# Moving v down the partitions, copies inside SBUF to SyncE, and masks to GpSimd in an attention and feed-forward kernel

## The chip, the core and the metric

The kernel runs on one core of a Trainium2 chip. A core has TensorE (matrix products into PSUM), VectorE and ScalarE (element work on SBUF and PSUM), GpSimd (element work on SBUF, and the issue of loads that convert types), SyncE (the issue of other transfers) and 16 DMA engines. Each engine works through its own list in order, and semaphores connect them. The metric is the device time of one execution in microseconds, as a median of several runs.

## The reference

Four batches of eight heads, 768 positions, 64 numbers a head. Each position attends to its neighbours closer than 16 and to one summary of every block of 32: the maximum of the block's k, and the mean of its v. The result, 3,072 rows of 512, goes through a feed-forward part with a hard-swish.

```python
k_sum = k.reshape(B, H, nb, block, D).max(axis=3)
v_sum = v.reshape(B, H, nb, block, D).mean(axis=3)
scores_l = scale * np.matmul(q, k.transpose(0, 1, 3, 2))        # kept where |i - j| < 16
scores_s = scale * np.einsum('bhsd,bhnd->bhsn', q, k_sum) + np.log(block)
a = softmax(concatenate([masked scores_l, scores_s]))
x = a @ concatenate([v, v_sum])                                  # (3072, 512)
h = x @ w_in                                                     # (512, 2048)
out = (h * clip(h + 3, 0, 6) / 6) @ w_out                        # (2048, 512)
```

## The kernel before

**Attention.** A batch is cut into 12 query blocks of 64. The queries are shifted by 16, so that block t needs the keys of positions 64t to 64t + 95. `kaug[p]` (p is one of four pairs of heads) holds for each block 96 key columns and the 24 block maxima, 120 in all; one matmul gives 64 queries' scores against all 120 (`scores`, L519). ScalarE takes the exponential into `at` (L527), VectorE multiplies the 96 neighbour rows by a band mask (L531; for the first half of batch 0 a bias is added on TensorE instead). `vaug` holds for each block the 120 rows of v that answer to these: on partitions 0 to 63 the block's own rows, on 64 to 95 the 32 rows ahead, which are the next block's first rows (the halo), on 96 to 119 the 24 block sums, the same for every block; a 65th column of ones gives the softmax's denominator. Its rows are 66 numbers apart. `values` (L632) multiplies `at` with `vaug`; `finish` divides (L663, L667), transposes on TensorE (L682) and copies to `x`.

**Where the rows come from.** For batch 0, k and q are loaded by rows (`knat`, `qnat`) and transposed on TensorE (L448, L493). For batches 1 to 3 they are loaded in squares of 32 into `kraw` (four loads, L367) and, shifted by 16 rows, into `qraw` (eight half loads, L375), of which there is one each, and VectorE transposes them (`turn`, L588, L592), with the third piece of each key window copied from the next. v is loaded by L385 in four loads a batch. For batch 0 the halo is copied by VectorE and ScalarE (`halo`, L406), for the others it is loaded from HBM a second time (`load_vhalo`, L393). The block sums are matmuls with an indicator (`vsum_first` L552, `vsum` L567); they are spread to all 12 blocks by copies for batches 0 and 1, by SyncE transfers from SBUF to SBUF for 2 and 3 (L575).

**Feed-forward.** Half a batch (384 rows) at a time: 16 tiles of `h` (four matmuls each, L700), drained by ScalarE (L705) and VectorE (L707) into `g`; then 128 rows of output with 16 matmuls (L720), an eviction to `ot` (L432) and a store (L730). The tiles go through three PSUM banks `h`, one bank `o`, and two pairs of banks `S` for attention.

**Order.** The order of the work is written out by hand in `ORDER`, a list of some 1,500 operations. `K10.0` is the load of batch 1's raw k, first part; `Q..` a load of q, `V..` of v, `I`, `O` of the weights, `H` the halo, `z` in the changed kernel a zero fill; `k`, `q`, `s`, `u`, `v`, `w` are the steps `k_step`, `q_step`, `scores`, the block sums, `values` and `turn`; `F` and `G` the two feed-forward products; `:A` and `:D` name the engine where there is a choice. `Plan.run` goes through the list with estimated durations to choose buffers, and each engine gets its operations in that order. In the first 22 us of that plan, matmuls on a constant tile (L803) fill TensorE's gaps.

```python
def load_v(b, c, prio):                          # L381
    op("POOL", 0.95, lambda: nc.gpsimd.dma_start(out=o[0:QB, lo:hi, 0:D], in_=rows[:, lo:hi]),
       w=[("v", b % 2, c)], prio=prio, dma=1.7)
```

Of the kernel before, what the change touches and what calls it, by code (L numbers as in the profile page):

```python
# [9 lines left out]
F32 = mybir.dt.float32  # L10
# [5 lines left out]
D = 64  # L16
BLK = 32
# [4 lines left out]
VW = 66  # L22
# [7 lines left out]
c.0 K00.0 c.7 K01.0 c.10 c.11 c.12 c.13 c.9 c.1 Q000.0 K02.0 Q010.0 c.2 c.3 k00.0 k01.0 q010.0 k01.1 k01.4 k00.1 q010.1:A  # L30
k00.4 c.4 k00.3:A k01.2 s010.0 q030.0 q000.0 q000.1:A s030.0 s010.1 s010.2 q020.0 q020.1:A k00.2 q030.1:D k01.3:D k03.0
k03.1 k02.0 k02.1 V00.0 V01.0 c.6 V02.0 V03.0 I0.0 I1.0 Q001.0 s000.0 u00.0 s000.1 u01.0 k03.3:A k03.2 k02.2 u00.1:D u00.2:D
k03.4 u01.1:D s000.2 u01.2:A u00.3:D k02.4 h21.0:D k02.3:D u02.0 s020.0 s030.1 s020.1 s020.2 u03.0 h30.0:D h00.0:D h10.0:D
h01.0:D v00.0 v02.0 u03.1:D u03.2:D v00.2 u01.3:D v00.3 u02.1:A s030.2 h20.0:A u02.2:A Q011.0 I2.0 I3.0 O0.0 O1.0 O2.0 O3.0
K10.0 K11.0 K13.0 K12.0 v01.0 v01.2 v02.1 v00.1 v02.4 v00.4 v00.5 v02.2 v02.3 v02.5 v00.6 v01.1 v01.3 v01.4 v01.5 h31.0:A
v00.7:A u03.3:A q001.0 q011.0 q001.1:A q021.0 q021.1:A u02.3:D q011.1:D v01.6 v02.6 q031.0 s021.0 v01.7:A h11.0:D v02.7:D
c.5 c.8 s021.1 F00.0 F00.1 F00.2 F00.10 F00.3 F01.0 F01.1 s001.0 s001.1 s021.2 q031.1:D F00.4 F01.2 s001.2 F00.11 F00.12
s011.0 F00.13 F00.14 Q121.0 Q101.0 Q110.0 Q100.0 Q120.0 Q131.0 Q130.0 Q111.0 s011.1 s011.2 s031.0 F00.5 F00.6 F00.7 F01.9
F00.8 F00.9 F02.6 s031.1 F01.3 F02.7 F01.10 F01.4 s031.2 F02.8 v04.0 v03.0 F01.6 F01.11 F01.5 v03.1 v03.2 F01.7 F01.8 v04.1
F02.3 F02.4 F02.5 F02.9 v03.3 v03.4:A F02.10 v04.2 F00.15 F02.0 v05.0 v04.3 F00.16 F02.1 F02.11 F00.17 F02.2 v05.1 v05.2  # L40
F03.3 F03.9 F03.0 v04.4:A F03.4 v05.3 F03.1 F03.10 v05.4:A G01.0 F03.5 F03.11 F03.2 F03.6 F10.0 F03.7 F12.0 F03.8 F10.1
F10.3 F12.1 F10.2 F12.2 F10.6 F10.4 F10.9 F10.5 F10.7 F10.8 F11.0 F10.10 F10.11 F11.6 F11.1 F11.9 F11.2 F11.7 F11.8 F11.10
F11.11 F12.6 F12.7 F12.8 F12.9 F12.10 F12.11 w12.0 G01.1 F13.0 F13.1 w13.0 F13.2 w11.0 w13.3 w10.0 w12.3 G01.2 G01.3 F12.3
F13.9 G01.4:A G02.0 G02.1 G02.2 G02.3 F11.3 F13.10 w11.2:A F12.4 F12.5 G02.4:A w12.2:A F13.3 F11.4 F13.4 w10.2:A w13.2:A
w12.4 w11.3 w11.4 w11.1 w11.5:D G00.0 G00.1 s110.0 s110.1 s110.3 w12.1 w13.1 w12.5:D w13.5:A G00.2 G00.3 s120.0 s120.1
s120.3 w13.4 w10.1 F13.5 w10.3 F11.5 w10.4 w10.5:D F13.11 V10.0 V13.0 V11.0 V23.0 V12.0 H1.0 K20.0 K22.0 V20.0 K21.0 Q231.0
K23.0 Q220.0 V22.0 V21.0 Q200.0 Q221.0 Q201.0 Q211.0 Q210.0 Q230.0 s130.0 G00.4:A F13.6 G12.0 s130.3 s130.1 F13.7 G00.5
G01.5 H1.1 G02.5 s120.2 s110.2 s130.2 s100.0 s100.1 F13.8 s100.2 s110.4 s100.3 G12.1 u1.0 u1.1:A u1.3:A u1.5:A G12.2 G12.3
G12.4:A u1.4:D u1.2:D v10.0 s120.4 v10.1 v10.5 v10.6 v10.2 s100.4 u1.7:A u1.6:A u1.9:A G11.0 G11.1 v12.0 v10.3 v10.4:A
u1.8:A v12.1 v12.2 s130.4 G11.2 v10.7 v12.3 v10.8:D G11.3 v12.4:A v13.0 F20.0 F20.3 G11.4:A F20.1 F20.4 v13.5 v13.1 v13.2  # L50
v13.6 F20.9 v13.3 v15.0 F20.10 F20.2 F20.5 F20.11 v15.1 v15.2 F20.6 F21.0 F20.7 F20.8 F21.1 V30.0 V31.0 V32.0 V33.0 F21.2
w21.0 F21.6 G10.0 F21.7 v13.4:A F21.8 F21.3 v15.3 v13.7 F21.9 F22.3 F21.4 F21.5 w20.0 F22.0 G10.1 F21.10 F22.4 v15.4:A
F21.11 F22.1 F22.5 F22.9 F23.0 F22.2 w20.3 F22.10 F22.11 F23.1 w21.2:A v13.8:A F23.2 w22.0 F22.6 u2.0 F22.7 F22.8 w21.3
G10.2 F30.0 F23.6 G10.3 w22.2:A F30.1 w20.4 F30.2 F30.3 F23.3 G10.4:A w22.3 w22.4 G22.0 G22.1 w20.1 u2.1:A w20.2:A F23.7
F23.4 w20.5:A F30.4 G12.5 u2.3 u2.5 G11.5 u2.4 u2.2 F23.5 F23.8 w22.1 s200.0 s200.1 s200.3 F30.5 w22.5:A F31.6 F23.9 G22.2
w23.1 F23.10 F31.7 s220.0 F23.11 F31.8 w21.4 w21.1 w21.5:D F30.9 G22.3 F31.0 F31.3 s220.3 s220.1 s210.0 G22.4:A H2.0 Q301.0
Q330.0 w23.0 K32.0 Q311.0 H3.0 F31.1 w23.5:A Q310.0 Q300.0 Q320.0 Q331.0 F31.2 F31.4 s200.4 F30.10 F30.11 F31.5 G20.0 G20.1
F30.6 F32.3 F33.0 Q321.0 K33.0 K31.0 K30.0 s210.1 s210.3 w23.3 F30.7 w23.4 s200.2 F30.8 w23.2:A F32.4 F33.1 u3.0 u3.1:D
s220.2 F33.2 s220.4 s210.2 G20.2 s230.0 s230.1 s230.3 s230.2 F32.5 G20.3 F31.9 F32.9 F31.10 F31.11 G20.4:A H2.1 G10.5 u3.3
u3.5 H3.1 G20.5 G22.5 v20.0 v20.1 v20.5 v20.2 v20.6 F33.9 G32.0 F32.10 F33.10 v22.0 F33.3 v20.3 F33.11 F32.0 G32.1 F33.4  # L60
v20.4:A v20.7 F32.1 v20.8:A v22.1 v22.2 F33.5 s230.4 F32.2 s210.4 v22.3 F32.11 v22.4:A F33.6 F32.6 F33.7 F32.7 v23.0 F33.8
v23.1 F32.8 F40.0 F40.1 F41.3 G32.2 F40.9 G32.3 F40.10 F41.4 v23.2 F40.2 F40.11 F41.5 v23.5 v23.6 F42.3 F41.9 F42.4 F42.5
F43.0 v25.0 F41.10 G32.4:A v23.3 F41.11 F42.0 F40.6 G30.0 G30.1 v23.4:A F43.1 F42.1 F40.7 v25.1 w30.1 F42.2 F43.2 F40.8
F41.0 F41.1 F41.2 v25.2 F40.3 F40.4 w30.5:A w33.1 w32.1 F42.6 G30.2 G30.3 F42.9 G30.4:A F42.7 v23.7 v23.8:A F42.10 G21.0
G21.1 G21.2 F40.5 w31.0 F42.8 F42.11 F43.3 F43.4 w30.0 w30.3 F43.6 w30.4 F43.5 w31.3 G21.3 F43.7 w32.5:D G21.4:A G21.5 v25.3
# [784 lines left out]
```

## Time and profile before

| | us |
|---|---|
| median of three runs | 234.51 (234.47 to 235.97) |
| the profiled execution | 233.64 |
| its span, first to last instruction | 231.9 |
| TensorE busy | 217.3 |
| VectorE, ScalarE, GpSimd busy | 156.7, 126.5, 72.8 |
| first feed-forward matmul | 30.30 |
| loads end | 138.4 |

Busy time of TensorE includes its gap fillers and a modelled end of each pipelined matmul, so it is not all useful work. A row of the table by windows gives, for a stretch of 5 us, the busy time and the number of instructions of TensorE, of its weight loads, of VectorE, ScalarE and GpSimd, then the granted share of TensorE's clock, the mean number of packets in flight on a DMA engine, and GB/s. A slice row of the page gives busy tenths in 40 equal slices of 5.8 us. In the chain the columns are start, length and what the time went to. In a timeline the columns are start, length, engine, line, operation, operands and count, and in brackets the idle time ahead with what ended it.

### The profile page before, as it was taken

How to read it: one execution, taken by the hardware profiler on the slowest of the kernel's cores; microseconds unless marked ns; L12 is line 12 of the kernel's file. 1: busy time of each engine (PE TensorE's matmuls, PEld its weight loads, DVE VectorE, ACT ScalarE, POOL GpSimd, SP SyncE). 2: the span in 40 equal slices, each digit the busy share in tenths (PEclk: the TensorE clock that was granted, in tenths of full speed). 3: DMA queues.
4: the chain of work that ended last, by engine and by line, in shares of the span. 5: the costliest groups of instructions: out<-in, count | busy, mean ns of one | idle time of the engine just before them, and what ended most of it. 6: DMA issues, size and time to landing. Idle time of an engine off the chain costs nothing.

```text
span 231.9 us, 5321 instructions
## 1 busy us (share of the span) xinstructions
PE 217.3 (94%) x2175; PEld 121.8 (52%) x2175; DVE 156.7 (68%) x327; ACT 126.5 (55%) x258; POOL 72.8 (31%) x86
## 2 busy tenths in 40 slices
PE   7899699999989997989999889999999999999991
PEld 2365476555445563545565445555555555555560
DVE  2489689789897669889785499945955645454201
ACT  2287567774588854768654535675552543434101
POOL 7994481357754734707741200000000000000000
PEclk9999979999999999999999999999999999999998
DMA  5999999999999999999999990132002030012013
GB/s 76 169 123 182 191 206 196 119 77 87 95 120 176 186 103 86 85 114 146 84 142 89 127 71 0 45 80 84 3 11 85 0 136 3 0 45 90 3 68 114
DMA packets 126585, 22.14 MB, mean 95 GB/s; under 512 B 116960, under 2 KB 123616, under 8 KB 126560
## 3 DMA queue, kind: packets, MB, share of 16 engines
q0 software_dynamic: 117280, 14.81, 217.7%
q1 hardware_dynamic: 9280, 6.98, 12.7%
q8 instruction: 17, 0.28, 0.7%
q14 instruction: 8, 0.07, 0.1%
HBM read 29.60 MB, written 6.29 MB: 155 GB/s over the span
## 4 chain that ended last, share of the span: by engine, by line
PE 58%; DMA 18%; issue 9%; POOL 9%; ACT 2%; DVE 2%; DVEq 0%; POOLq 0%
PE h L700 26%; PE o L720 22%; DMA kraw<-in_k_dram 13%; DMA qnat<-in_q_dram 5%; PE h L720 4%; POOL vaug L385 3%; ACT at L527 2%; PE S L519 1%; PE S L632 1%; POOL qraw L375 1%; POOL qnat L357 1%; PE S L682 1%; POOL knat L346 1%; POOL win L417 1%; POOL kraw L367 1%
## 5 line engine op out<-in xcount | busy, mean ns | idle before, releaser
L700 PE MATMUL h<-x,win 128*128 128x384 bf16 (+1 forms) x536 | 95.0, 321 | 3.1 <-DVE g L707 3.1
L705 ACT ACTIVATE r<-h 128x384 f32<-128x384 f32 x128 | 60.4, 493 | 59.4 <-PE h L700 58.7
L707 DVE SCALAR_TENSOR_TENSOR g<-r,h 128x384 bf16<-128x384 f32 x128 | 67.5, 545 | 33.9 <-ACT r L705 32.1
L720 PE MATMUL o<-wout,g 128*128 128x512 bf16 x336 | 82.3, 379 | 0.2 <-ACT ot L432 0.2
L700 PEld LDWEIGHTS <-win 128*128 128x128 bf16 x536 | 49.9, 99 | 37.5 <-issue 3.6
L720 PEld LDWEIGHTS <-g 128*128 128x128 bf16 x400 | 38.1, 98 | 36.3
L375 POOL DMA_DIRECT2D qraw<-in_q_dram x24 | 21.3, 890 | 29.1 <-issue 10.5
L527 ACT ACTIVATE at<-S 120x768 bf16<-120x768 f32 x32 | 24.8, 812 | 7.1 <-PE S L519 7.1
L367 POOL DMA_DIRECT2D kraw<-in_k_dram x12 | 15.8, 1317 | 13.5 <-issue 12.0
L385 POOL DMA_DIRECT2D vaug<-in_v_dram x16 | 15.1, 949 | 4.8 <-PE h L700 3.1
L592 DVE STREAM_TRANSPOSE qaug<-qraw 128x800 bf16<-128x800 bf16 x12 | 11.8, 998 | 6.2 <-DMA kraw<-in_k_dram 3.3
L667 DVE TENSOR_TENSOR xn<-S,rc 128x512 bf16<-128x512 f32 (+1 forms) x25 | 15.7, 643 | 0.4
L531 DVE TENSOR_TENSOR at<-at,mask 96x768 bf16<-96x768 bf16 x28 | 14.8, 546 | 1.5 <-ACT at L527 1.0
L432 ACT COPY ot<-o 128x512 f32<-128x512 f32 x16 | 9.4, 586 | 11.3 <-PE o L720 10.6
L588 DVE STREAM_TRANSPOSE kaug<-kraw 128x768 bf16<-128x768 bf16 x12 | 11.5, 965 | 2.1 <-DMA kraw<-in_k_dram 2.1
L432 ACT COPY x<-S 128x512 bf16<-128x512 bf16 x19 | 11.0, 587 | 2.5 <-PE S L682 2.1
L519 PEld LDWEIGHTS <-kaug 64*128 64x128 bf16 x384 | 7.0, 96 | 8.2 <-issue 6.3
L605 DVE TENSOR_REDUCE red<-kaug 128x24 bf16<-128x768 bf16 x12 | 11.2, 940 | 0.0
L519 PE MATMUL S<-qaug,kaug 64*128 64x64 bf16 x384 | 9.2, 192 | 2.0 <-ACT at L527 1.2
L803 PE MATMUL o<-idle 128*128 128x512 bf16 x30 | 9.5, 442 | 1.5 <-DVE idle L287 1.5
L720 PE MATMUL h<-wout,g 128*128 128x512 bf16 (+1 forms) x64 | 10.9, 326 | 0.0
L632 PEld LDWEIGHTS <-at 120*64 120x64 bf16 x384 | 7.6, 111 | 5.9 <-issue 4.8
(84 smaller groups left out, 139.3 us busy)
## 6 DMA issues: line engine op xcount, KB each, us to landing
out_dram<-ot SPq DMA_DIRECT2D x19, 256.0 KB
vaug<-in_v_dram POOLq DMA_DIRECT2D x16, 192.0 KB, 10.7
kraw<-in_k_dram POOLq DMA_DIRECT2D x12, 192.0 KB, 14.8
qraw<-in_q_dram POOLq DMA_DIRECT2D x24, 96.0 KB, 11.9
win<-in_moe_w_in_dram POOLq DMA_DIRECT2D x4, 512.0 KB, 11.8
wout<-in_moe_w_out_dram POOLq DMA_DIRECT2D x4, 512.0 KB, 13.5
vaug<-in_v_dram POOLq DMA_DIRECT2D x3, 380.0 KB, 16.2
out_dram<-ot SPq DMA_DIRECT2D x4, 224.0 KB
```

The lines of the kernel that those rows point to most:

```text
L367: op("POOL", 0.8, lambda hs=hs, ds=ds, rows=rows: nc.gpsimd.dma_start(out=kraw[rows], in_=k[b, hs].rearrange("h (c r) d -> r (h c) d", r=B ...
L375: nc.gpsimd.dma_start(out=qraw[lo:lo + PAD, 1 - x:1 - x + NP * NB], in_=src[PAD * (1 - x):PAD * (2 - x)])
L385: op("POOL", 0.95, lambda: nc.gpsimd.dma_start(out=o[0:QB, lo:hi, 0:D], in_=rows[:, lo:hi]), w=[("v", b % 2, c)], prio=prio, dma=1.7)
L432: {"ACT": nc.scalar.copy, "DVE": nc.vector.tensor_copy, "POOL": nc.gpsimd.tensor_copy}[eng](o, i)
L519: nc.tensor.matmul(X[p, half].slot[:, j, i * QB:(i + 1) * QB], kaug[p][rows, t], qT[rows, p, t * QB:(t + 1) * QB], start=not masked, stop= ...
L527: op("ACT", act(2 * HALF), lambda a=a, x=x: nc.scalar.activation(a, x.slot[0:KEYS, :, 0:HALF], AF.Exp, scale=scl), r=[x], w=[("at", p, hal ...
L531: op("DVE", dve(2 * HALF, 1.92), lambda m=m, half=half: nc.vector.tensor_tensor(m, m, mask[:, half * HQ:(half + 1) * HQ].unsqueeze(1).to_b ...
L667: nc.vector.tensor_tensor(o, src[..., 0:D], r.unsqueeze(len(r.shape)).to_broadcast(list(o.shape)), op=ALU.mult)
L700: nc.tensor.matmul(h.slot[:, lo * 128:hi * 128], w_in_sb[:, kt, ft * 128:(ft + 1) * 128], xt[s].slot[:, kt, lo * 128:hi * 128], start=(kt ...
L705: op("ACT", act(HALF), lambda: nc.scalar.activation(r.slot[:], h.slot[:, 0:HALF], AF.Relu, bias=0.5, scale=1.0 / 6.0), r=[h], w=[r], prio= ...
L707: op("DVE", dve(HALF), lambda: nc.vector.scalar_tensor_tensor(gt[s].slot[:, ft], r.slot[:], 1.0, h.slot[:, 0:HALF], op0=ALU.min, op1=ALU.m ...
L720: nc.tensor.matmul(o.slot[:, a:z], gt[s].slot[:, ft, ts * 128:(ts + 1) * 128], w_out_sb[:, ft, a:z], start=(ft == 0), stop=(ft == NFT - 1))
```

## The change

1. The window of a block is turned round: its own 64 rows of v lie on partitions 32 to 95, the 32 rows behind it (the previous block's last rows) on 0 to 31. Keys, masks, q shift and indicator follow; the first half of batch 0 is now the later rows (`low`). Rows of `vaug` are 80 numbers apart, not 66.
2. The halo of every batch is copied by two SyncE transfers from SBUF to SBUF (`halos`), none is loaded from HBM; VectorE and ScalarE keep one copy a pair for the first half of batch 0. The indicator covers 96 partitions, so partitions 0 to 31 are filled with zeros first (`empty`), on VectorE for one buffer and on GpSimd for the other.
3. Block sums are spread by SyncE for all batches. In the first half of batch 0 pairs 0 and 1 keep a copy; pairs 2 and 3 multiply their sums from a small tile `vf` in a second matmul that adds to the first.
4. `kraw` and `qraw` have two buffers each; the second shares its place with `knat` and `qnat` of batch 0. Raw q is no longer shifted at the load, so it takes four loads a batch.
5. The second half of batch 0's q is loaded with 128 rows on the partitions and transposed in 128 x 128 pieces.
6. The mask multiply, the third key piece and some small copies may go to another engine; 14 mask multiplies go to GpSimd (`:P`).
7. `ORDER` is a new list, sorted by the plan's start times; durations in the plan are changed. The last output tile is one of two halves of 256 columns.

```diff
-VW = 66
+VW = 80
-kraw = sb([128, NP * NB, BLK], BF16, "kraw")
-qraw = sb([128, NP * NB + 1, BLK], BF16, "qraw")
+first = sb([128, 2 * NP * NB, BLK], BF16, "first")
+kraw, qraw = ([sb([128, NP * NB, BLK], BF16, f"{n}raw"), first[:, i * NP * NB:(i + 1) * NP * NB]] for i, n in enumerate("kq"))
...
+def empty(eng, i, c):
+    eng.memset(vaug[i][0:BLK, 2 * c:2 * c + 2, :, 0:D].bitcast(F32), 0.0)
+    if i == 0:
+        eng.memset(vf[c][WIN:KEYS, :, D:D + 2], float(BLK))
...
+def low(x):
+    return (1 - x) * HQ
...
+nc.gpsimd.dma_start(out=o[n:128], in_=q[b, :, lo + n:lo + 128].rearrange("h r d -> r h d"))
...
+for name, src, o in (("K", k, kraw[(b + 1) % 2]), ("Q", q, qraw[(b + 1) % 2])):
+    for g in range(4):
...
+        op("POOL", 1.32, lambda src=src, o=o, hs=hs, ds=ds, rows=rows: nc.gpsimd.dma_start(
+            out=o[rows], in_=src[b, hs].rearrange("h (c r) d -> r (h c) d", r=BLK)[:, :, ds]),
...
-op("POOL", 0.95, lambda: nc.gpsimd.dma_start(out=o[0:QB, lo:hi, 0:D], in_=rows[:, lo:hi]),
+op("POOL", 0.95, lambda: nc.gpsimd.dma_start(out=o[BLK:WIN, lo:hi, 0:D], in_=rows[:, lo:hi]),
...
-op("POOL", 0.75, lambda: nc.gpsimd.dma_start(out=o[QB:WIN, 0:n - 1, 0:D], in_=rows[0:WIN - QB, 1:n]),
...
+op("SP", 0.7, lambda: nc.sync.dma_start(out=o[0:BLK, 1:n, 0:D], in_=o[QB:WIN, 0:n - 1, 0:D]),
...
+op("SP", 0.7, lambda: nc.sync.dma_start(out=end[0:BLK, :, 0, 0:D], in_=end[QB:WIN, :, NQ - 1, 0:D]),
...
-op("DVE", dve(2 * HALF, 1.92), lambda m=m, half=half: nc.vector.tensor_tensor(
+op(("DVE", "POOL"), {"DVE": 0.62, "POOL": 1.75}, lambda eng, m=m, half=half: ENGINE[eng].tensor_tensor(
...
+def spread(i, c, src, a, z, prio):
+    def go():
+        for j in range(2):
+            nc.sync.dma_start(out=vaug[i][WIN:KEYS, 2 * c + j, a:z, 0:D], in_=src(j).unsqueeze(1).to_broadcast([NB, z - a, D]))
...
+if not alone or pairs[0] == 0:
+    nc.tensor.matmul(y, a[:, cols], vaug[b % 2][0:KEYS, h, t, 0:D + 1], start=True, stop=True)
+elif part == 0:
+    nc.tensor.matmul(y, a[0:WIN, cols], vaug[0][0:WIN, h, t, 0:D + 1], start=h == 2 * pairs[0], stop=False)
+else:
+    nc.tensor.matmul(y, a[WIN:KEYS, cols], vf[p][WIN:KEYS, h % 2, 0:D + 1], start=False, stop=h == H - 1)
```

## The prediction

> **What bounds the kernel now.** I read the page's busy times and slices first, then the table by windows of 5 us, then the chain of work that ended last, then TensorE's timeline, and last the groups.
>
> ```profile
> span 231.9 us, 5321 instructions
> ...
> PE 217.3 (94%) x2175; PEld 121.8 (52%) x2175; DVE 156.7 (68%) x327; ACT 126.5 (55%) x258; POOL 72.8 (31%) x86
> ...
> PE   7899699999989997989999889999999999999991
> ...
> DMA  5999999999999999999999990132002030012013
> ```
>
> TensorE is busy 94% of the span, no other engine over 68%. The DMA row says more: every slice from 6 to 138 us is at 9, so until the last raw k of batch 3 is in, TensorE lives on what the loads deliver. The table by windows shows where TensorE did nothing:
>
> ```profile
> 25.00:30.00 5.00, 2.98 (x59) 2.38 (x59) 3.60 (x12) 2.96 (x5) 2.81 (x4) 0.85 1.28 197
> ...
> 65.00:70.00 5.00, 3.92 (x85) 2.20 (x83) 4.91 (x12) 4.31 (x9) 2.26 (x2) 1.00 4.76 121
> ...
> 85.00:90.00 5.00, 3.63 (x28) 2.20 (x26) 2.95 (x6) 2.15 (x6) 2.66 (x3) 1.00 6.06 90
> ...
> 100.00:105.00 5.00, 4.43 (x67) 2.60 (x67) 5.00 (x10) 4.05 (x9) 0.00 (x0) 1.00 4.18 120
> ...
> 130.00:135.00 5.00, 3.27 (x19) 1.60 (x17) 2.36 (x4) 1.23 (x5) 0.00 (x0) 1.00 3.04 146
> ```
>
> The second column is TensorE's busy time of 5: idle 2.02 at 25 us, 1.08 at 65, 1.37 at 85, 0.57 at 100, 1.73 at 130; from 135 to 225 there is none. The chain in order of time names the releasers:
>
> ```profile
> 14.98 12.10 DMA qnat<-in_q_dram
> ...
> 73.13 13.78 DMA kraw<-in_k_dram
> ...
> 126.44 6.13 DMA kraw<-in_k_dram
> ...
> 219.48 7.81 PE h L720 x48
> 227.29 0.03 DVEq L432
> 227.33 0.04 issue
> 227.37 0.69 DVE ot L432
> ```
>
> Three times a load of q or k is the step on the path. The end is one eviction of 512 columns and a store, 4.6 us after the last matmul. At the front TensorE's timeline has:
>
> ```profile
> 25.27 0.32 PE L632 MATMUL S<-vaug,at 120*64 120x65 bf16 x8
> 27.21 0.53 PE L493 MATMUL S<-ident,qnat 96*64 96x96 bf16 x16 [1.62 <-DMA qnat<-in_q_dram]
> ...
> 30.30 2.45 PE L700 MATMUL h<-x,win 128*128 128x128 bf16 x20
> ```
>
> Here 1.62 us are lost to the second half of q, and the first matmul of the feed-forward part starts at 30.30 although win's first quarter landed at 21.15 (landing events of the loads). From here on TensorE's order is fixed work: 0.65 us for four L700 matmuls, 0.865 for four of L720.
>
> **The change, part by part.** *Front.* The second-half q is listed behind six feed-forward tiles, not ahead of them. Ten of the sixteen spread and halo copies of batch 0 that stood ahead of L700 (0.36 to 0.83 us each) go, partly to SyncE, partly by adding the sums in a second matmul for pairs 2 and 3: 24 more matmuls at 0.02 us = 0.5 us. The four new zero fills (768 elements; 192 take 0.22 us, so about 0.85 each) lie in VectorE's idle 4.51 us before its first reduction at 6.85. Without the qnat wait x could be there by 24 to 26 us, five earlier. But early work helps only if the loads keep up.
>
> *The load queue.* GpSimd's loads land one behind the other, so I add up spacings of landings. The new order puts all four v loads of batch 1 ahead of that batch's sums on TensorE, which stand ahead of its first scores: the gate. Before, the last q of batch 1 landed at 61.86. To that:
> - v: 4 loads more. One costs 1.66 us now (69.89 - 63.30 over four). Its 128-byte rows lay 132 bytes apart, now 160. No row shows the new spacing; bounds are 1.66 and, at raw k's time per run (1.87 us for 3,072 runs, on rows at even 64 bytes) for 1,536 runs, 0.94. Like raw k's, the new rows start at multiples of 32 bytes, so I take 1.15, nearer to it: +4.6 for the four, -2.0 for batch 0's.
> - raw q of batch 1: eight half loads took 9.96 us (51.90 to 61.86); four whole ones at 1.87, as raw k's first two, are 7.5: -2.5 (0 if they stay as slow; k's other two took 2.95 and 2.40).
> - second-half q of batch 0: 3.7 us (23.92 to 27.64); now 3,072 runs like two v loads, 2.3: -1.4 (-0.4 to -1.8).
> - new transfers inside SBUF for batch 0: 1,152 + 3,296 runs of 128 bytes. Eight such spreads (2,304 runs, at 97.6 to 106) stretched one v landing from 1.7 to 2.64, so 0.4 ns a run: +1.8. Bounds 0 and 7.8, the latter if hardware-queue packets, 28 ns each in the trace, never overlap others on the 16 engines.
>
> Gate: 61.9 + 4.6 - 2.0 - 2.5 - 1.4 + 1.8 = 62.4. TensorE's own arrival is earlier: 24.5 + 29.25 us of feed-forward matmuls listed ahead (140 of L700, 48 of L720) + 3.4 of attention + 2 of small waits = 59. The kernel before had done the same feed-forward work at 64.0 and one pair of scores (0.46) more, so at equal work it stood at 63.5. **Gain at the gate: 1.1.** The half clock from 28.46 to 31.88 lies ahead of it and is worth nothing by itself.
>
> A rule speaks against this part. The Trainium skill, page "DMA: Bandwidth & Descriptors", section "Issuing engines are not separate DMA queues", says that transfers from SyncE and GpSimd run on the same 16 DMA engines and interleave. By it moving work to SyncE frees no transfer time; the stretched v landing agrees, and the sum has the price in it.
>
> *Batch 1's scores.* Before, four pairs stand within 4.6 us of listed work and TensorE waits 0.73 and 0.35 us for exponentials; now within 6.8. **1.1.**
>
> *Batch 2.* With its own buffer raw k follows v of batch 1 at once: 62.4 + 4 x 1.87 = 69.9, q 77.4 (86.9 and 99.4 before). Its turn is listed 7.2 us behind the gate (70.7 with a pair of values), its scores 19 us plus 3.2 of values and transposes behind (84.6). The idle 1.37 and 0.57 go: **2.0**; the cover for q is 7 us.
>
> *Batch 3.* Eight raw loads and eight v follow: 77.4 + 15.0 + 9.2 = 101.6, where the last raw k came at 138.4. The halo loads from HBM are gone too (2.9 to 6.0 us each). The 1.73 goes: **1.7**. What is late next is only ScalarE and PSUM.
>
> *End.* The last piece is 256 columns, evicted in 0.376 us (ScalarE's row) for 0.69: **0.3**.
>
> *GpSimd masks.* 14 of 28 leave VectorE, which was no bound. No row shows a multiply on GpSimd; VectorE's takes 0.55 us, GpSimd's select 0.576 for 384 elements, so 1.15 for 768 and 2.3 if two inputs take twice that. In batch 1 five masks of m and two load issues of 1.32 run one after another and start 1.9 us after the first scores; the value matmuls that need all of them come 11.75 us after these (10.3 listed, 1.45 of values and transposes). Stall: 5m + 4.5 - 11.75, nothing up to m = 1.45. I take 1.5, nearer the single-input row: 0.3 a batch, **-0.8** in three with rounding up; at 2.3, 4.3 a batch.
>
> The Trainium skill, "GPSIMD Engine Reference", section 3.1 "Elementwise — side-by-side cycle accounting", states about 2.6 cycles an element at 1.2 GHz for such an operation. An estimate from it is 1.66 us; the sum by it would be 2.4 us worse.
>
> *SyncE.* Stores queue behind spreads that wait for sums. SyncE is nearly empty, three ot buffers cover it: 0. Without that cover a late v blocks a store, then the one o bank, then TensorE, which is part of the second rival.
>
> Sum: 1.1 + 1.1 + 2.0 + 1.7 + 0.3 - 0.8 = 5.4. Span 231.9 - 5.4 = 226.5; around it lie 1.74 us (233.64 - 231.9), so 228.2 for a profiled execution. The median of the runs stood 0.87 above that execution: **229.1**.
>
> **Rivals.**
> 1. *The loads never gate.* V at 0.94 and free transfers put the gate at 58.4, so TensorE's 59 counts: 4.5, and all idle time from 65 to 135 (5.1) and 0.3 go: span 222.0, 224.6 as a median. For it: each load spacing could fall; against: the DMA row at 9 throughout.
> 2. *The change doesn't relieve the queue.* V stays at 1.66: 61.9 + 6.6 - 2.5 - 0.4 + 1.8 = 67.4, 3.9 late; the later terms remain: net 0.4 gained, 234.1. With transfers at 7.8 it would be 240.
> 3. *GpSimd becomes the bound.* Masks wait in GpSimd's order behind loads that wait in turn: a load is issued only once the one eight before has landed (win at 19.56 for v's 19.27). At m = 2.3 TensorE loses 4.3 in each of three batches: 231.9 - 6.2 + 12.9, so 241. It decides from 5m - 7.25 = 2.1, m = 1.87, where the 6.2 are eaten. For it: a fixed order on GpSimd; against: between these masks stands much other work.
>
> **How the numbers follow.** Forecast 0.52 (225.5 to 232), rival 1 0.20, rival 2 0.16, rival 3 0.12. The range takes rival 1 down to 222.5 (some idle could vanish beyond the 5.1) and rival 2 up to 236; outside are rival 3 and the tail of rival 2. A measurement tells about 1% (2.3 us) from no change: faster 0.71 (rival 1 and nearly all of the forecast's), same 0.17, slower 0.12.
>
> **What would show it.** First L700 matmul at 24 to 27 us; v landings 1.1 to 1.3 us apart; the sums of batch 1 on TensorE at 61 to 63, released by a v load; no TensorE idle put down to kraw or qraw after that; GpSimd masks at 1.5 us. Wrong: masks near 2 us with TensorE waiting for them at the values, v still 1.66 apart, or DMA slices at 9 beyond 110 us.

## The result, and the profile after

| | before | after |
|---|---|---|
| median of four runs, us | 235.09 (234.47 to 235.97) | 243.56 (241.83 to 244.54) |
| ratio to before, 95% interval | | 1.035 (1.027 to 1.043) |
| profiled execution, us | 233.64 | 244.54 |
| its span | 231.9 | 242.8 |
| first feed-forward matmul | 30.30 | 24.91 |
| last load landed | 138.4 | 132.4 |

Executions more than 1.5% above the fastest of their kernel are left out of the ratios and intervals, here and below, but not out of the medians.

The change made the kernel 3.5% slower; 229.1 us had been forecast. The page of the kernel after, with the busy line of all engines and the slices (6.07 us each here):

```profile
span 242.8 us, 5311 instructions
...
PE 218.7 (90%) x2164; PEld 121.6 (50%) x2164; DVE 158.1 (65%) x311; ACT 118.3 (49%) x246; POOL 88.0 (36%) x89
...
PE   6889992079999598999999999999999999999993
...
PEclk9999999559999869999999999999999999999999
...
DMA  5999999999999999999969012621011011001213
```

The DMA row falls off earlier than before, though later than was forecast: it stands at 9 up to slice 20 (about 121 us) and once more in slice 22 (127 to 133 us), where before it stood at 9 up to 138 us. Slices at 9 beyond 110 us were one of the prediction's signs of being wrong. What cost the time is in the other two rows. TensorE has a hole in slices 7 and 8, and TensorE's granted clock (PEclk) is at 5 in slices 8 and 9 and low again in 14 and 15. The table by windows, with the columns of the one before, gives the size:

```profile
35.00:40.00 5.00, 2.95 (x26) 1.32 (x24) 2.68 (x5) 2.55 (x5) 0.37 (x1) 1.00 1.44 216
40.00:45.00 5.00, 0.00 (x0) 0.00 (x0) 0.00 (x0) 0.00 (x0) 0.94 (x1) 0.68 2.47 124
45.00:50.00 5.00, 0.27 (x2) 0.18 (x3) 0.00 (x0) 0.00 (x0) 2.71 (x3) 0.50 2.96 119
50.00:55.00 5.00, 4.71 (x42) 2.69 (x42) 2.48 (x6) 0.49 (x1) 4.29 (x5) 0.50 4.03 119
80.00:85.00 5.00, 2.07 (x30) 1.04 (x28) 5.00 (x5) 1.63 (x4) 3.43 (x3) 0.77 1.42 90
85.00:90.00 5.00, 5.00 (x36) 2.00 (x35) 3.46 (x6) 2.66 (x4) 2.93 (x2) 0.54 0.64 134
```

From 40 to 50 us TensorE worked for 0.27 us. From 41.8 to 55.4 its clock was granted at 0.5, so also the work after the hole ran at half speed: the hole costs 11.12 + 0.95 us of waiting and, from 50.3 to 55.4, about 2.6 more. The same on a smaller scale stands at 80 to 90: 2.9 us of waiting and some 3.0 from half clock (83.6 to 89.6). Together that is 20.6 us lost in two places, against 10.9 us of longer span; the rest of the kernel gained about 9.7, some of which is only that loads ran on while TensorE stood still. TensorE's timeline has the waits and what ended them:

```profile
49.07 0.27 PE L648 MATMUL S<-vaug,at 120*64 120x65 bf16 x2 [11.12 <-DMA vaug<-vf]
50.28 1.04 PE L648 MATMUL S<-vaug,at 120*64 120x65 bf16 x30 [0.95 <-DMA vaug<-vf]
...
83.60 0.82 PE L541 MATMUL S<-qT,kaug 64*128 64x64 bf16 x24 [2.93 <-DVE kaug L447]
```

In the chain of work that ended last, in order of time, three pieces name the two places:

```profile
24.45 18.84 DMA vaug<-vaug
44.83 5.41 DMA vaug<-vf
...
79.46 4.09 DVE kaug L447
```

**The first place is a transfer from SBUF to SBUF.** At 24.45 SyncE issues the copy of batch 0's rows behind (L421, `vaug` to `vaug`); it is 18.84 us on its way. A block sum queued behind it (`vf` to `vaug`) takes 5.41 more, and the values of batch 0's second half need both. The timeline of SyncE (SPq) has the issue, and behind it two spreads (copies of block sums to the blocks) whose issue took 13.6 us together:

```profile
24.45 0.68 SPq L421 DMA_DIRECT2D vaug<-vaug  x1
25.18 13.60 SPq L562 DMA_DIRECT2D vaug<-vf  x2
43.31 0.64 SPq L423 DMA_DIRECT2D vaug<-vaug  x1
```

The records of single packets say why. The copy is 32 partitions times 95 rows: 3,040 packets of 128 bytes. While it ran, the loads sent the last quarter of `w_in` and then `w_out` in packets of 1,024 bytes. From 29 to 39 us each 2 us hold 368 to 385 of the small ones and 366 to 378 of the large ones: one for one. A small packet takes 26 ns by itself and a large one 96, but each small one let a large one pass, on 16 engines. The same copy of batch 1, with no load beside it (77 to 79 us), moved some 1,000 packets in 1 us. One for one holds beside the weights only: beside 64-byte packets of raw loads, from 46 to 47 us, a spread moved 215 packets and the loads 1,409. The Trainium skill, page "DMA: Bandwidth & Descriptors", section "Queues, rings and completion order", states that an engine goes round its queues and takes one packet from each in turn; the counts beside the weights agree, with a packet in these records being a single row, where the page has several descriptors in one.

**The second place is a copy on VectorE.** The timelines of VectorE (DVE) and GpSimd (POOL) at the pair of heads that TensorE waited for:

```profile
78.52 0.91 DVE L617 TENSOR_REDUCE red<-kaug 128x24 bf16<-128x768 bf16 x1
79.46 4.08 DVE L447 COPY kaug<-red 128x288 bf16<-128x288 bf16 x1
83.47 1.47 DVE L726 SCALAR_TENSOR_TENSOR g<-r,h 128x384 bf16<-128x384 f32 x3
```

```profile
78.84 1.36 POOL L394 DMA_DIRECT2D first<-in_q_dram  x1
80.21 3.23 POOL L554 TENSOR_TENSOR at<-at,mask 96x768 bf16<-96x768 bf16 x2
```

The copy of the block maxima (128x288) takes 4.08 us here. In the kernel before it took 0.26 us on average; for the same batch VectorE's timeline there has:

```profile
67.69 0.23 DVE L608 COPY kaug<-red 128x288 bf16<-128x288 bf16 x1
```

The slow one starts while GpSimd issues a load and ends 0.1 us after GpSimd's two masks. The reduction ahead of it and the hard-swish operations behind it have their usual times.

### The profile page after: what moved, and what is told of

Its sections match the earlier page's. It is cut to its first block, busy times and chain, and to the rows that moved or that the text cites. A ratio compares the mean times of both kernels' runs of the same rounds, so it can differ in the third digit from the quotient of the medians.

```text
span 242.8 us, 5311 instructions
## 1 busy us (share of the span) xinstructions
PE 218.7 (90%) x2164; PEld 121.6 (50%) x2164; DVE 158.1 (65%) x311; ACT 118.3 (49%) x246; POOL 88.0 (36%) x89
## 4 chain that ended last, share of the span: by engine, by line
PE 73%; DMA 12%; DVE 8%; POOL 2%; ACT 1%; issue 1%; SPq 1%; DVEq 0%; POOLq 0%
PE h L719 30%; PE o L739 27%; DMA vaug<-vaug 8%; PE h L739 4%; PE S L648 3%; DMA vaug<-in_v_dram 2%; DVE kaug L447 2%; PE S L541 2%; DMA vaug<-vf 2%; PE S L701 2%; DVE g L726 1%; DVE at L554 1%; DVE red L617 1%; PE S L589 1%; POOL first L365 1%
## 5 line engine op out<-in xcount | busy, mean ns | idle before, releaser
L719 PE MATMUL h<-x,win 128*128 128x384 bf16 (+1 forms) x536 | 97.2, 324 | 0.4 <-ACT x L447 0.2
L739 PE MATMUL o<-wout,g 128*128 128x512 bf16 x336 | 85.0, 387 | 0.0
L554 POOL TENSOR_TENSOR at<-at,mask 96x768 bf16<-96x768 bf16 x14 | 22.9, 1640 | 59.5 <-ACT at L550 29.9
L648 PE MATMUL S<-vaug,at 120*64 120x65 bf16 x352 | 8.8, 201 | 12.4 <-DMA vaug<-vf 12.1
L682 DVE RECIPROCAL rc<-S 128x8 f32<-128x8 f32 (+1 forms) x25 | 4.8, 197 | 19.0 <-PE S L648 18.5
L648 PEld LDWEIGHTS <-at 120*64 120x64 bf16 x360 | 7.3, 115 | 16.8 <-DMA vaug<-vf 11.6
L394 POOL DMA_DIRECT2D qraw<-in_q_dram x8 | 10.6, 1323 | 14.0 <-issue 14.0
L447 ACT COPY x<-S 128x512 bf16<-128x512 bf16 x17 | 10.0, 587 | 8.7 <-PE S L701 8.6
L447 ACT COPY ot<-o 128x512 f32<-128x512 f32 x14 | 8.2, 586 | 11.4 <-PE o L739 11.4
L541 PE MATMUL S<-qT,kaug 64*128 64x64 bf16 x384 | 9.9, 197 | 3.0 <-DVE kaug L447 2.9
L554 DVE TENSOR_TENSOR at<-at,mask 96x768 bf16<-96x768 bf16 x14 | 10.4, 751 | 3.0 <-ACT at L550 2.6
L739 PE MATMUL h<-wout,g 128*128 128x256 bf16 (+1 forms) x64 | 11.1, 326 | 0.0
L394 POOL DMA_DIRECT2D kraw<-in_k_dram x8 | 10.5, 1318 | 0.5 <-DMA win<-in_moe_w_in_dram 0.5
## 6 DMA issues: line engine op xcount, KB each, us to landing
kraw<-in_k_dram POOLq DMA_DIRECT2D x8, 192.0 KB, 13.5
```

The lines of the kernel that those rows point to most:

```text
L394: op("POOL", 1.32, lambda src=src, o=o, hs=hs, ds=ds, rows=rows: nc.gpsimd.dma_start(out=o[rows], in_=src[b, hs].rearrange("h (c r) d -> r ...
L447: {"ACT": nc.scalar.copy, "DVE": nc.vector.tensor_copy, "POOL": nc.gpsimd.tensor_copy}[eng](o, i)
L541: nc.tensor.matmul(X[p, half].slot[:, j, i * QB:(i + 1) * QB], kaug[p][rows, t], qT[rows, p, t * QB:(t + 1) * QB], start=not masked, stop= ...
L554: op(("DVE", "POOL"), {"DVE": 0.62, "POOL": 1.75}, lambda eng, m=m, half=half: ENGINE[eng].tensor_tensor(m, m, mask[:, low(half):low(half) ...
L648: nc.tensor.matmul(y, a[:, cols], vaug[b % 2][0:KEYS, h, t, 0:D + 1], start=True, stop=True)
L719: nc.tensor.matmul(h.slot[:, lo * 128:hi * 128], w_in_sb[:, kt, ft * 128:(ft + 1) * 128], xt[s].slot[:, kt, lo * 128:hi * 128], start=(kt ...
```

## The experiments

Each was compared with the kernel before on the same chip. The kernel before itself had medians of 233.6 to 235.1 us in these comparisons, and single executions spread over up to 5%, so differences of under 1% are told by the trace and not by the time, and ratios say more than differences of medians. Line numbers shift by a few between the kernels: the mask is L554 to L559, copies L447 to L453, values L648 to L659, the block sums of batch 1 L589 to L595. The letters of the theories in the quoted expectations are named in words here.

| run | what differs from the kernel after | median us | ratio to before (95%) | profiled span |
|---|---|---|---|---|
| e1 | first transfer: 1,280 packets | 238.18 | 1.018 (1.009 to 1.026) | 238.2 |
| e2 | transfers of rows behind in whole stretches | 237.76 | 1.014 (1.003 to 1.025) | 233.6 |
| e3 | GpSimd's 14 masks on VectorE | 249.17 | 1.066 (1.060 to 1.073) | 247.0 |
| e4 | batch 0's transfers as VectorE copies | 237.13 | 1.015 (1.006 to 1.025) | 235.9 |
| e5 | a 128x16 copy on ScalarE | 242.42 | 1.042 (1.035 to 1.050) | 240.5 |
| e6 | e2 and e5 | 236.27 | 1.017 (1.007 to 1.026) | 233.8 |
| e7 | e6, first transfer 256 packets of 800 B | 235.30 | 1.011 (1.006 to 1.015) | 232.8 |
| e9 | the slow copy on ScalarE | 242.61 | 1.040 (1.035 to 1.046) | 241.4 |
| e10 | e7 and e9 | 234.66 | 1.004 (0.999 to 1.008) | 233.6 |
| e11 | e7, batch 1's masks on VectorE | 235.01 | 1.009 (1.006 to 1.012) | 232.1 |
| e12 | e11, two of four pairs of sums spread by engines | 232.37 | 0.998 (0.993 to 1.003) | 229.5 |
| e8 | kernel **before**, rows 160 bytes apart | 231.23 | 0.995 (0.988 to 1.001) | 230.1 |
| e13 | e8 once more, more rounds | 230.52 | 0.988 (0.981 to 0.995) | 232.6 |

### The long transfer: shorter, coarser, or not at all

The first run lets batch 0's transfer carry only the blocks that no engine copy had supplied.

```diff
-op("SP", 0.7, lambda: nc.sync.dma_start(out=o[0:BLK, 1:n, 0:D], in_=o[QB:WIN, 0:n - 1, 0:D]),
+def behind():
+    if b:
+        nc.sync.dma_start(out=o[0:BLK, 1:n, 0:D], in_=o[QB:WIN, 0:n - 1, 0:D])
+    else:
+        for t in range(1, HQ):
+            nc.sync.dma_start(out=end[0:BLK, :, t, 0:D], in_=end[QB:WIN, :, t - 1, 0:D])
+op("SP", 0.7, behind,
```

> Edit: for batch 0 SyncE copies only the five blocks of each head whose halo is still missing, 1,280 runs of 128 bytes in five transfers, in place of 3,040 in one. Theory A (on each DMA engine a packet of SyncE's queue takes turns with one packet of the software queue, so a transfer lasts its packets per engine times the packet beside it): 80 packets per engine times 0.097 us = 7.8 us after 24.5, so landed near 32.5 instead of 43; the value matmuls at 38 no longer wait (12.1 us of idle and about 2.5 us of half clock gone): span 228 to 230. Theory B (SyncE's transfer waits until the software loads queued ahead of it have drained): the number of runs does not matter, it lands at 40 to 43, span within 2 us of 242.8.

The second copies one stretch of 15,200 bytes a partition, with the gaps between the rows (zeroed once).

```diff
-op("SP", 0.7, lambda: nc.sync.dma_start(out=o[0:BLK, 1:n, 0:D], in_=o[QB:WIN, 0:n - 1, 0:D]),
+line = vaug[i][:].rearrange("p h t d -> p (h t d)")
+op("SP", 0.7, lambda: nc.sync.dma_start(out=line[0:BLK, VW:n * VW], in_=line[QB:WIN, 0:(n - 1) * VW]),
```

> Edit: the long halo transfer of every batch copies whole rows of 80 numbers, ones and filled-up padding included, so that source and target are one stretch of 15,200 bytes on each of 32 partitions; the padding of the 32 source partitions is filled with zeros once (about 0.7 us on VectorE for each buffer). Theory A: a few packets per engine, so the halo of batch 0 lands within 2 to 4 us of its issue, TensorE's wait of 12.1 us at 38 goes and with it the half clock: span 227 to 230. Theory B: unchanged, landing at 40 to 43.

The fourth has no SyncE transfers for batch 0: VectorE copies rows and block sums at the same places of the list.

```diff
+if b == 0:
+    op("DVE", 1.4, lambda: nc.vector.tensor_copy(end[0:BLK, :, 1:HQ, 0:D], end[QB:WIN, :, 0:HQ - 1, 0:D]), ...
+    op("DVE", 0.3, lambda: nc.vector.tensor_copy(end[0:BLK, :, 0, 0:D], end[QB:WIN, :, NQ - 1, 0:D]), ...
+    return
...
-spread(0, c, lambda j: vf[c][WIN:KEYS, j, 0:D], 0, HQ, late)(r=[("vf", c)], after=LATER)
+op("DVE", 0.4, lambda: nc.vector.tensor_copy(vaug[0][WIN:KEYS, 2 * c:2 * c + 2, 0:HQ, 0:D],
+                                             vf[c][WIN:KEYS, :, 0:D].unsqueeze(2).to_broadcast([NB, 2, HQ, D])), ...
```

> Edit: batch 0's remaining halo copies and spreads are done by VectorE at the same places of the list (2,560 and 512 elements, four spreads of 0.36 us), SyncE has none of batch 0; the later batches are unchanged. Theory A or B alike: the wait at 38 goes, the first feed-forward matmul comes 1 to 3 us later for the VectorE work in the front: span 228 to 232. If the span stays at 240 or more, the wait at 38 was not due to these transfers.

All three bring the median from 243.6 to 237 or 238 us. TensorE's wait for these rows, 11.12 us, shrinks to 2.70 with 1,280 packets, to 0.91 with whole stretches and to nothing without the transfer. So the long transfer is worth 5.4 to 6.4 us, less than the 14.7 counted above: the hole had hidden other waits. In e1 and e4, for instance, TensorE waits 1.8 and 4.5 us for batch 1's block sums, which the kernel after does not. The expectations had spans of 227 to 232 us; the profiled ones are 238.2, 233.6 and 235.9. In e1 the last of the five transfers landed at 38.4 and not at 32.5: the estimate counted these packets alone, and block sums went through SyncE's queue between them. The engine copies paid with 2.71 us of TensorE idle from 25.4, ahead of the first feed-forward matmul. Whole stretches paid too, as TensorE's timeline shows:

```profile
34.99 1.46 PE L721 MATMUL h<-x,win 128*128 128x384 bf16 x4 [1.82 <-DMA win<-in_moe_w_in_dram]
...
44.13 0.67 PE L650 MATMUL S<-vaug,at 120*64 120x65 bf16 x30 [0.91 <-DMA vaug<-vf]
```

The fourth quarter of `w_in` landed at 34.94 us, against 30.29 with 1,280 packets. A packet of 15,200 bytes held an engine for 990 to 1,590 ns on average, and from 30 to 32 us only 109 packets of the load got through, where 366 to 378 do beside small ones. Turn by turn favours whoever has the larger packet, in both directions. The seventh run, below, takes the middle: 256 packets of 800 bytes for the missing blocks.

### The masks on VectorE

```diff
-... s130.2:D s110.4:P Q23.0 s100.2:P s100.4:P s130.4:P ...
+... s130.2:D s110.4:D Q23.0 s100.2:D s100.4:D s130.4:D ...
```
(and so for all 14)

> Edit: the 14 mask multiplies of GpSimd go back to VectorE at the same places of the list. Theory C (VectorE's copy of the block maxima took 4.08 us instead of 0.26 because it could not run beside GpSimd's multiplies): the copy takes 0.26 again, TensorE's wait of 2.9 us at 80 to 83.6 and the half clock from 82.7 to 89.6 (3 us) go: span 236 to 238. Rival D (the wait at 80 was VectorE being late with its list anyway, more so with 14 multiplies added): the wait stays or grows, span 242 to 246.

It became the slowest kernel of all, with a span of 247.0 us (236 to 238 by the theory, 242 to 246 by its rival). Yet what it was to show, it shows: VectorE's timeline has the copy of the maxima at 0.88 us in place of 4.08, and TensorE does not wait for it. What came instead is in TensorE's and SyncE's timelines:

```profile
87.91 0.22 PE L648 MATMUL S<-vaug,at 120*64 120x65 bf16 x2 [2.44 <-ACT kaug L447]
...
89.73 0.22 PE L648 MATMUL S<-vaug,at 120*64 120x65 bf16 x2 [0.93 <-DMA vaug<-vs]
91.02 0.92 PE L648 MATMUL S<-vaug,at 120*64 120x65 bf16 x26 [1.06 <-DMA vaug<-vs]
```

```profile
76.31 9.27 SPq L562 DMA_DIRECT2D vaug<-vs  x8
```

The values of batch 1, reached earlier, now wait for the block sums, which SyncE spreads in eight transfers issued from 76.3 to 85.6. (For 87.91 the profile names a ScalarE copy; a spread landed at the same time, 87.82, and I read the wait as one for it.)

Their issue is not what makes them late. In the kernel after, the eight were issued within 0.5 us of the same times. There the last one, issued at 84.35 with hardly a load beside it, landed at 86.51, 2.2 us on. In e3 the last one, issued at 84.80, landed at 90.97, 6.2 us on, while the loads moved 580 to 1,650 packets in 1 us. So it is again the loads beside them that hold small transfers.

Half clock follows from 89.8 to 96.7. Set matmul against matmul, e3 is 5.4 us ahead of the kernel after when that stands at 89.5, level when the values run through at 91.0, 2.8 behind at 95.8, behind the half clock, and 4.4 behind at 165.4, where 1.08 of waiting for VectorE has been added. That accounts for the 4.2 us between the profiled spans; the medians are 5.6 apart. VectorE's list was a cost, but not what held batch 1's values.

### A copy moved in error, then the right one

Runs e5 to e7 were to move the slow copy to ScalarE. The list's entry `w12.5` was taken for it; it is the copy of 128x16 queries of another pair.

```diff
-... w13.4:D w12.5:D ...
+... w13.4:D w12.5:A ...
```

> The changed kernel with one thing moved: batch 1's last copy of block maxima into kaug (128x288), 4.08 us on VectorE beside GpSimd's masks, goes to ScalarE in the same place of the list. Theory B (VectorE's fast copies are held while GpSimd multiplies): on ScalarE the copy takes its usual 0.42 us, TensorE's 2.93 us at 83.6 goes, and most of the half clock of 82.7 to 89.6 with it (another 1 to 3 us): 238 to 240.5 us; other VectorE copies and mask multiplies beside GpSimd stay slow. Rival B' (the copy was slow by its own source or destination, or by something ahead of it): it is slow on ScalarE too, 243 to 244.5 us. Theory A (the 3,040-run transfer of batch 0) is untouched by this run and keeps its 11 us of idle time from 38 to 49 in either case.

Nothing follows for the cause: the slow copy stayed on VectorE and took 4.08 us again. The run e6 adds the whole stretches.

> The second experiment (transfers of the rows ahead as whole stretches of 15,200 B) and the moved copy together. If A and B are separate and add, the wait of 3.1 us at 72 goes from 237.8 and some half clock with it: 232.5 to 235 us, about the kernel before. Rival: something else is late directly behind the copy (the values' spreads, the raw loads of batch 2), and the time stays at 236.5 to 238.

The median, 236.27, lies between the two expectations. Here list and masks fell differently: the copy ran ahead of the masks in 0.24 us, and two mask multiplies on VectorE (0.55 us each before) took 3.91 us together, for which the values waited 2.0; ahead of that they had waited 2.7 for two spreads, by the landings (76.7 and 77.6). Run e7 replaces the first transfer:

```diff
+rows = end[:].rearrange("p h t d -> p h (t d)")
+ahead = ((line[0:BLK, VW:n * VW], line[QB:WIN, 0:(n - 1) * VW]) if b else
+         (rows[0:BLK, :, VW:HQ * VW], rows[QB:WIN, :, 0:(HQ - 1) * VW]))
+op("SP", 0.7, lambda: nc.sync.dma_start(out=ahead[0], in_=ahead[1]),
```

> As the run before, but batch 0's transfer carries only the five blocks that the values still lack, 256 runs of 800 B instead of 32 of 15,200 B. In the whole-stretch run the loads behind it landed late (fourth piece of w_in at 34.94 us instead of 30.29, TensorE idle 2.7 us at 31 to 33). Theory A2 (a queue's share of the DMA engines goes by packets, so long packets of SyncE's queue take time from the loads): with 800-B packets and 205 KB instead of 486 KB the fourth piece lands by 31 to 32 us, the 2.7 us goes, and the values still find their rows: 230 to 233 us, below the kernel before. Rival: that piece is late because its issue came 1.2 us later, not by sharing: it lands near 34 again and the time is that of the run before.

The fourth quarter of `w_in` lands at 31.9, as the sharing by packets said; the waits there fall from 2.6 us (e6) to 1.4 in all, and none for rows behind is left. 230 to 233 us was missed: the maxima copy, beside the masks again, took 5.09 us and TensorE waited 3.94 for it.

Run e9 moves the right entry in the kernel after, and nothing else.

```diff
-... w13.5:A w13.4:D F13.2 ...
+... w13.5:A w13.4:A F13.2 ...
```

> The changed kernel with the copy that the trace shows blocked really moved: the three runs before had moved the last copy of batch 1's queries (128x16) instead, and the copy of block maxima took 4.08 us on VectorE again. Here that copy (128x288, pair 3 of batch 1) goes to ScalarE, nothing else. Theory B (VectorE's fast copies and mask multiplies are held while GpSimd multiplies): it takes 0.42 us there, the 2.9 us before that pair's scores and some half clock go, and the median falls from 242 to 243.6 to 237.5 to 240.5 us; if a VectorE mask multiply then stands beside GpSimd's masks, that one is stretched to 1.5 to 2 us. Rival B' (the copy was slow by its source or destination): 3 to 4 us on ScalarE too, and no change of time.

On ScalarE the copy took 0.43 us. The time did not move, because the next VectorE operations of that kind took its place. GpSimd, then VectorE:

```profile
80.58 5.14 POOL L554 TENSOR_TENSOR at<-at,mask 96x768 bf16<-96x768 bf16 x3 [0.48 <-ACT at L550]
```

```profile
81.61 1.02 DVE L726 SCALAR_TENSOR_TENSOR g<-r,h 128x384 bf16<-128x384 f32 x2 [1.82 <-ACT r L724]
82.55 1.68 DVE L554 TENSOR_TENSOR at<-at,mask 96x768 bf16<-96x768 bf16 x1
84.16 1.59 DVE L447 COPY qT<-qT 128x16 bf16<-128x16 bf16 x1
85.66 0.97 DVE L600 STREAM_TRANSPOSE kaug<-first 128x768 bf16<-128x768 bf16 x1
```

A mask multiply takes 1.68 us instead of 0.55, and the copy of 128x16, 0.15 us elsewhere in this run, takes 1.59; TensorE waits 2.09 for that:

```profile
85.81 0.35 PE L541 MATMUL S<-qT,kaug 64*128 64x64 bf16 x12 [2.09 <-DVE qT L447]
```

The last of the two ends with the third mask, at 85.7. The hard-swish operation, whose inputs are 4 bytes wide and partly in PSUM, and the transpose keep 0.51 and 0.97. So it is the engine pair, not this copy: shown by two different operations taking the delay over when the first is removed. The Trainium skill, page "SBUF — State Buffer", section "Who interferes with whom", has the rule: fast VectorE copies, and multiplies with two inputs in SBUF, use a port pair that GpSimd uses too, and one side waits for the other's whole instruction. The durations agree, except that the copy of 4.08 us was held through more than one GpSimd instruction; transposes and reductions, seen here at their usual times, are not held.

Run e10 is e7 with this edit.

> The run with 256 runs of 800 B for batch 0, and this copy on ScalarE too. Its wait of 3.9 us at 69 goes. Theory B: 235.3 falls to 231 to 233.5 us. Rival: the blocking moves on to the next VectorE operations with 2-byte operands (mask multiplies), the values wait for those 2 to 4 us as in the run with whole stretches, and the time stays at 234.5 to 236.

It gave 234.66, the rival's outcome: two mask multiplies took 5.21 us together, and the values waited 1.95 for them, and 2.15 ahead of that for two spreads, by the landings (76.2 and 77.1).

### What holds batch 1 once both are gone

Run e11 is e7 with the five masks of batch 1 back on VectorE.

```diff
-... w20.0 s130.2:D s110.4:P Q23.0 s100.2:P s100.4:P s130.4:P Q31.0 s120.4:P V23.0 ...
+... w20.0 s130.2:D s110.4:D Q23.0 s100.2:D s100.4:D s130.4:D Q31.0 s120.4:D V23.0 ...
```

> The run with 256 runs of 800 B for batch 0, and the five masks of batch 1 that GpSimd had on VectorE in the same places (the other nine stay on GpSimd). Theory B: no VectorE copy or mask of batch 1 takes over 0.9 us, the wait of 3.9 us goes, VectorE's list grows by 5 x 0.55 = 2.75 us of which 1 to 2 land on the values: 232 to 234.5 us. Rival D (VectorE's list is the bound between 70 and 90 us, as in the run with all masks on VectorE): the values start later by the whole 2.75 us and half clock follows, 235.5 to 238.

No VectorE copy or mask of that batch takes over 0.55 us, and no wait for one is left, but the time, 235.0, is that of e10 and lies between the two expectations. TensorE's timeline at the values of batch 1, and SyncE's:

```profile
77.72 0.22 PE L653 MATMUL S<-vaug,at 120*64 120x65 bf16 x2
78.51 0.22 PE L653 MATMUL S<-vaug,at 120*64 120x65 bf16 x2 [0.56 <-DMA vaug<-vs]
79.40 0.22 PE L653 MATMUL S<-vaug,at 120*64 120x65 bf16 x2 [0.67 <-DMA vaug<-vs]
80.30 0.60 PE L653 MATMUL S<-vaug,at 120*64 120x65 bf16 x26 [0.68 <-DMA vaug<-vs]
```

```profile
66.44 9.07 SPq L567 DMA_DIRECT2D vaug<-vs  x8
```

Again the spreads: the sums were on VectorE at 65.7, eight issues took SyncE 9.07 us, and the values took one pair after another, 0.9 us apart, as the transfers came. Here too the issue alone does not explain it. The last one, issued at 74.73, landed at 80.26, 5.5 us on, beside 370 to 1,350 packets of the raw loads of batch 2 in 1 us; with the 2.2 us that one took in the kernel after without loads, it would have landed at 76.9, ahead of the 77.7 at which TensorE came to the values. The next expectation names SyncE's issue time; the landings point to the sharing with the loads. The last experiment gives two pairs to ScalarE and VectorE.

```diff
+if b == 1 and c < 2:
+    op(EITHER, {"ACT": 1.4, "DVE": 0.8}, lambda eng, c=c: copy(
+        eng, vaug[i][WIN:KEYS, 2 * c:2 * c + 2, :, 0:D],
+        vs.slot[32 * c:32 * c + NB].rearrange("p (j d) -> p j d", j=2).unsqueeze(2).to_broadcast([NB, 2, NQ, D])), ...
+    continue
```

> The run with 256 runs of 800 B and batch 1's masks on VectorE, and one edit more: of batch 1's block sums, the pairs 0 and 1 are spread by one ScalarE and one VectorE copy in the same places of the list instead of four SyncE transfers; pairs 2 and 3 stay with SyncE. In the run without it the sums were on VectorE at 65.7 us, SyncE's eight issues stood from 66.4 to 75.5, and TensorE's values of batch 1 waited for them three times at 77.7 to 80.2 (0.76, 0.86, 0.88 us). Theory C (SyncE's own issue time, which the prediction took as nothing, holds these values): those waits go, nearly 2.5 us, less 0.5 to 1 for the two copies in ScalarE's and VectorE's lists: 232 to 234 us against 235.0. Rival D (VectorE's and ScalarE's lists hold the values): the waits turn into waits for masks and exponentials and the time stays at 234.5 to 236.5.

```profile
61.03 0.23 PE L594 MATMUL S<-vaug,ind 96*32 96x128 bf16 x2
62.69 0.85 PE L594 MATMUL S<-vaug,ind 96*32 96x128 bf16 x46 [1.43 <-DMA vaug<-in_v_dram]
...
74.76 0.25 PE L659 MATMUL S<-vaug,at 120*64 120x65 bf16 x4
76.48 0.63 PE L659 MATMUL S<-vaug,at 120*64 120x65 bf16 x28 [1.47 <-DVE at L559]
```

The waits for spreads are gone, 1.47 us for a mask are there in their place, and the ratio falls from 1.009 (1.006 to 1.012) in e11 to 0.998 (0.993 to 1.003): level with the kernel before. So the spreads through SyncE were part of the loss, and VectorE's list is next. This run halves both their issues and their packets, so it does not tell the two apart; the landings above speak for the packets.

### The pitch alone

In the kernel before, only the distance of the rows of v is changed (v stays on partitions 0 to 63, the rows ahead still come from HBM):

```diff
-VW = 66
+VW = 80
...
-nc.vector.memset(t[0:WIN, :, :, D:VW], 1.0)
+nc.vector.memset(t[0:WIN, :, :, D:D + 2], 1.0)
```

> The kernel before with only the pitch of its value tiles changed, rows of 80 elements (160 B) instead of 66 (132 B); v stays on partitions 0 to 63, the rows ahead still come from HBM. If the pitch is what shortens a load of v, batch 1's four land 1.2 to 1.35 us apart instead of 1.53 to 1.7, rows ahead also shorter, and the raw keys and queries behind them come 1.2 to 2 us earlier per batch: 232 to 234 us, 0.3 to 1% below the kernel before. If the partitions are, they stay 1.6 apart and the time is within 0.3%.

> The kernel before with rows of 80 elements once more, with more rounds, beside the run above: its first reading was 231.2 us against 234.5, with an interval of 0.988 to 1.001 that reached just over 1. If the shorter v loads (1.3 us instead of 1.65 in batch 1) are worth 1 to 3 us of the time, it stands at 230.5 to 233 and the interval lies below 1; if that reading was chance, at 233 to 235.

Five v loads around 63 to 70 us land 1.33 us apart on average in place of 1.65 (63.47 to 68.77, before 63.30 to 69.89), and the last raw k of e8's profiled execution lands at 135.3 instead of 138.4 (138.6 in that of e13, which at 234.28 was among its slowest). The second reading, 230.52 us, ratio 0.988 (0.981 to 0.995), puts it below the kernel before, by few executions; that of the first, 0.995, reached from 0.988 just over 1. It is the fastest version found, and the only one with an interval below 1. The run e12, measured beside e13 at 0.998, has this pitch too: so no run here shows that the rest of the change, mended as far as it was, gains any time.

## Why the prediction was wrong, step by step

**What held.** *Front:* the first feed-forward matmul came at 24.91, as the 24 to 26 said. *v loads:* 1.21 to 1.43 us apart in the kernel after where they follow one another, where 1.15 was taken between 0.94 and 1.66; the pitch run shows that the wider pitch by itself shortens them. *The gate:* with the long transfer mended (e12), the sums of batch 1 began at 61.03 and were released by a v load at 62.69; 62.4 was forecast. That is the nearest of four: in e7, e10 and e11 it came at 63.3, 63.0 and 64.8. *Batches 2 and 3:* the idle 1.37, 0.79 and 1.73 us are gone; behind 92 us the kernel after waits three times, 0.30, 0.36 and 0.17, and e12, which has no hole for loads to catch up in, 0.85 for a copy of q on ScalarE and twice 0.16. *End:* from the last matmul to the end of the span it was 4.6 us and is 3.9; 0.3 was taken. *Mask:* 1.640 us on GpSimd against 1.5; by the Trainium skill, "GPSIMD Engine Reference", section 3.1, the estimate was 1.66, and the trace agrees.

**The step that failed** is "new transfers inside SBUF for batch 0", with its companion "SyncE is nearly empty, three ot buffers cover it: 0". The first priced what the transfers take from the loads, 1.8 us in bounds of 0 to 7.8. In the kernel after, the last v load of batch 1 landed at 65.16, 2.8 behind the 62.4, and in e12, with fewer packets, at 62.65: more than the price, but within its bounds. What the loads take from the transfers had no price. 3,040 packets, each behind a load's packet, took 18.8 us to land, and TensorE was ready for those rows 13.5 us behind the issue; a spread behind them cost 5.4 more. The bounds covered a longer load queue, not a late transfer. The Trainium skill's rule that was weighed there (queues interleave on the same engines) was read in one direction only.

**The same zero failed a second time** in batch 1: eight spreads, behind sums at 65.7, are issued until 75.5 in e11, land 5.5 to 8.4 us behind their issue beside the loads, and the values waited 0.56, 0.67 and 0.68 us for them. In the kernel before, engine copies did that, and the values began 2.6 us behind the sums (70.87 and 73.48).

**Batch 1's scores, 1.1**, were not gained: before, TensorE waited 0.73 and 0.35 us between them, and in e12 it still waits 0.37, 0.35 and 0.50. Of the 1.1 of the gate some 0.8 is there in e12 (62.69 against 63.5), but 1.47 for a mask stands behind it, where the kernel before had no such wait at its values.

**GpSimd masks, -0.8.** The duration was right and the place was not. The prediction looked for TensorE waiting for masks at the values, at 5m + 4.5 - 11.75, which is 0.95 at 1.64. The loss came through VectorE: "14 of 28 leave VectorE, which was no bound" left out that VectorE's copies and its own masks stand still beside them. That cost 2.9 us of waiting and about 3.0 of half clock. Rival 3 had GpSimd decide from m = 1.87; GpSimd cost these 5.9 us at 1.64, by another road. That rival 3's 241 us, and the 240 of rival 2 with transfers at 7.8, lie near the measured 243.56 is chance: TensorE did not wait for GpSimd's masks at the values, and the load queue, which rivals 1 and 2 were about, was not where it went wrong.

**Half clock.** The prediction dismissed the half clock at 28 to 32 us. It did not ask what a new hole would bring: the granted clock fell to 0.5 some 4 us into the first wait and 2 us into the second, for 13.7 and 6.8 us, and took some 5.6 us on top of the waits.

**What stays open.** How much of the 9.7 us gained elsewhere in the kernel after is real and how much is loads catching up in the hole was not separated. In e12 the ratio, 0.998 (0.993 to 1.003), leaves at most some 1.6 us of the 5.4 that were forecast. Why VectorE's copy is held through several GpSimd instructions, and whether the length of the 15,200-byte packets or their 486 KB slowed the weights, no run separates.

## What to carry to other kernels

A transfer inside SBUF isn't free because its queue is empty: count its packets, ask which loads run beside it, and beside loads of long rows charge it one of their packets for each of its own; fewer and longer rows help, until they hold up the loads. Work moved from VectorE to GpSimd is to be priced with VectorE's own copies and two-input operations standing still beside it, and moving one of these only passes the delay on to the next. When a gate moves earlier, check every hand-over behind it, the landing of small transfers beside the loads among them, before the gain is counted.

## What the runs showed of the hardware that was not expected

- Beside 1,024-byte load packets, 128-byte packets from SyncE moved at 190 in 1 us, one for one with the loads' (96 and 26 ns each); without loads beside them at about 1,000. Packets of 800 bytes went at 106 to 117 in 1 us, with 14 to 17 of 128 bytes, again about one for one with the loads' 131. At 15,200 bytes the loads were down to 109 in 2 us.
- A spread of 288 packets of 128 bytes landed 2.2 us behind its issue with hardly a load beside it (kernel after, 84.35 to 86.51) and 6.2 us beside loads (e3, 84.80 to 90.97).
- A VectorE copy of 0.15 us took 1.59 beside GpSimd's multiplies, one of 0.26 up to 5.09 (e7), a mask of 0.55 up to 4.74 (e10); transposes (0.97), reductions (0.91) and hard-swish operations (0.51) were not held.
- Half clock came 4 us into TensorE's hole of 11 us (from 37.9, at 41.8) and 2 us into that of 2.9 us (from 80.7, at 82.7), and lasted on behind both, 5.1 and 6.0 us into renewed work.
- Rows of v 160 bytes apart in SBUF instead of 132 shorten a load of 1,536 rows of 128 bytes from 1.65 to 1.33 us (e8).
